# The opening of an attention and feed-forward kernel, its first chunks ordered by hand

## The chip, the cores and the metric

The kernel runs on one core of a Trainium2 chip. The metric is the device time of one execution in microseconds (us), the median of several; lower is better. A core has a matrix engine (TensorE, PE in the profile), a vector engine (VectorE, DVE), an engine for functions (ScalarE, ACT), GpSimd (POOL), which here does little but issue loads, and SyncE (SP), which issues the stores.

## The reference

Attention with a local window and eight global keys for 4 batches of 8 heads, 768 positions of 64 values, followed by a feed-forward network with a squared ReLU on 3072 tokens of 512 values.

```python
scores = scale * np.matmul(q, k.transpose(0, 1, 3, 2))
rel = pos[:, None] - pos[None, :]
is_global = pos[None, :] < 8
is_local = (rel >= 0) & (rel < 96)
dist = np.where(is_global & ~is_local, 96., np.abs(rel))
scores = np.where(is_global | is_local, scores - slopes[h] * dist, -1e9)
a = softmax(scores);  x = (a @ v) as tokens x (heads * 64)
h = np.maximum(x @ w_in, 0.0)          # w_in 512 x 2048
out = (h * h) @ w_out                  # w_out 2048 x 512
```

Inputs and the output are float32; the loads turn the inputs into float16.

## The kernel before

The tokens are cut into 12 chunks of 256 (3 per batch). A chunk `c` has `u = c % 3`; for `u` other than 0 its attention also needs keys and values of the chunk before it and the global ones of its batch's first chunk.

What is done for one chunk:

- `load(c)`: three loads `sq`, `sk`, `sv` (256 KB each as float16) on GpSimd's DMA queue. The weights come on the same queue, `w_in_sb` and `w_out_sb` in four parts of 512 KB each. The queue's order is the order in which the code issues them. A new load waits for the landing of the one eight before it.
- `turn_q(c)`, `turn_k(c)` (together `prep(c)`): eight transposes each on TensorE into PSUM, then a copy out, on ScalarE, or on VectorE in the opening of chunk 0. For `qx` two half-copies follow on VectorE (`beside`). For `kx` with `u` other than 0 four VectorE copies exchange keys (`change`).
- `fix_v(c)`: copies of `sv` into `vodd` and `veven` on VectorE, one copy for `u = 0`, five otherwise.
- `attention(c)` gives eight jobs, `att[c][0..7]`. Jobs 0 and 1 (`both`) compute the scores of two pairs of heads each: 16 matmuls `sp`, four exponentials `ex` on ScalarE, then two products with the decay mask, `phat`, on VectorE. Jobs 2 to 5 (`attend`) are eight matmuls `av` each, then a reciprocal `rec` and a product `tm` on VectorE. Jobs 6 and 7 (`to_x`) are four matmuls `trx` and a cast `xt` on ScalarE. The usual order of the eight is 0, 2, 3, 1, 6, 4, 5, 7.
- `f1(c)`: eight jobs of the first layer, each eight matmuls `hps` (128 x 256), a ReLU `hr` on ScalarE and its square `h` on VectorE.
- `f2(c)`: eight jobs of the second layer, each four matmuls `yps` (128 x 512). They run through two halves of the tokens (j = 0, 1) and four parts of `w_out`. After the fourth job of a half a copy `y` on VectorE and the store follow.

The order of instructions on each engine is written out by hand. A list of main jobs (`f1`, `f2`) is mixed with side jobs by `place(main, side, slots)`: a side job with slot i stands ahead of main job i. `run` goes through such a list. VectorE work that follows a ScalarE result (`phat`, `h`, `beside`, `change`) is put in a list `later` and given out ahead of the next job.

The opening does the attention of chunk 0 and starts that of chunk 1. Then come three mixed lists: `f1(0)` with the attention of chunk 1, `f1(1)` with that of chunk 2, `f2(0)` with that of chunk 3. From there a loop takes for each chunk `c` the jobs of `f2(c)` and `f1(c + 1)` in turn, with the attention of chunk `c + 3` and the preparation of chunk `c + 4` beside them. `warm(n)` is n matmuls on zeros into a bank that nobody reads; before, there is one call with six.

PSUM has six banks in rotation for all of these tiles (`bank`), and two for `yps`. The masks are filled on ScalarE by `fill_decay`: first the part for chunks with `u = 0`, and later the third part, for chunks with `u` other than 0.

Of the kernel before, what the change touches and what calls it, by code (L numbers as in the profile page):

```python
# [10 lines left out]
AF = mybir.ActivationFunctionType  # L11
# [3 lines left out]
P = 128  # L15
# [3 lines left out]
def place(main, side, slots):  # L19

    out = []
    for i in range(len(main) + 1):
        out += [g for g, s in zip(side, slots) if s == i] + main[i:i + 1]
    return out
# [3 lines left out]
def kernel(  # L28
# [73 lines left out]

    def fill_small():
        V = nc.vector
        V.memset(tiny, 0.0)
        nc.scalar.activation(out=tiny, in_=tiny, func=AF.Exp)
        V.memset(zero, 0.0)
        V.memset(fill, BIG)
        V.memset(fill[0:GP, 0:1], float(NL))
        V.memset(fill[HP:HP + GP, 1:2], float(NL))  # L110
        V.memset(shift[0:HP], 0.0)
        V.memset(shift[HP:P], float(CH))
        V.memset(thr[0:HP], 0.0)
        V.memset(thr[HP:P], -float(P - 1))

    def fill_dist():

        V = nc.vector
        V.tensor_scalar(out=ident, in0=jmp, scalar1=0.0, scalar2=None, op0=ALU.is_equal)
        V.tensor_scalar(out=dist[:, 1, 0, :], in0=dist[:, 0, 0, :], scalar1=1.0,  # L120
                        scalar2=None, op0=ALU.subtract)
        V.tensor_scalar(out=dist[:, :, 1, :], in0=dist[:, :, 0, :], scalar1=float(P),
                        scalar2=None, op0=ALU.add)
        V.tensor_scalar(out=dist[:, :, 2, :], in0=dist[:, :, 0, :], scalar1=shift,
                        scalar2=None, op0=ALU.add)
        V.tensor_scalar(out=cut, in0=dist, scalar1=0.0, scalar2=float(NL - 1), op0=ALU.max,
                        op1=ALU.min)
        V.tensor_tensor(out=off, in0=dist, in1=cut, op=ALU.not_equal)
        for k0, k1, f in ((0, 2, 0), (2, 3, 1)):
            V.tensor_scalar(out=off[:, :, k0:k1, :], in0=off[:, :, k0:k1, :],  # L130
                            scalar1=fill[:, f:f + 1], scalar2=None, op0=ALU.mult)
        V.tensor_tensor(out=dist, in0=cut, in1=off, op=ALU.max)

    def fill_decay(k0, k1, h0, h1):
        for h in range(h0, h1):
            nc.scalar.activation(out=mask[:, :, h, k0:k1, :], in_=dist[:, :, k0:k1, :],
                                 func=AF.Exp, scale=-slopes[h])

    def fill_perm():
        nc.vector.tensor_scalar(out=perm, in0=jmp2, scalar1=thr, scalar2=None,  # L140
                                op0=ALU.is_equal)

    def warm(n):
        wps = bank([P, 512], "warm")
        for _ in range(n):
            nc.tensor.matmul(wps, lhsT=zero[:, 0:P], rhs=zero, start=True, stop=True)
# [2 lines left out]

    later = []  # L150

    def run(jobs):
        for job in jobs:
            todo, later[:] = list(later), []
            for f in todo:
                f()
            job()


# [9 lines left out]
    def load(c, *which):  # L169
        ck = chunks[c]  # L170
        for src in which or (q, k, v):
            if src is q:
                dst = ck.sq = stage_p.tile([P, H, P], FP16, name="sq", tag="sq")
            elif src is k:
                dst = ck.sk = stage_p.tile([P, H, P], FP16, name="sk", tag="sk")
            else:
                dst = ck.sv = sv_p.tile([P, H, P], FP16, name="sv", tag="sv")
            nc.gpsimd.dma_start(  # L178
                out=dst, in_=src[ck.b, :, ck.u * CH:(ck.u + 1) * CH, :].rearrange(
                    "h (p e) d -> p h (e d)", e=2))  # L180

    def turn_q(c, h0=0, h1=H, by=None):
        ck = chunks[c]
        if h0 == 0:


            ck.q = qk_p.tile([P, 3, H, P], FP16, name="qx", tag="qx")
        trp = bank([P, H, P], "trq", FP16)
        for h in range(h0, h1):
            nc.tensor.transpose(out=trp[:, h, :], in_=ck.sq[:, h, :], identity=ident)  # L190
        hh = slice(h0, h1)
        (by or nc.scalar.copy)(out=ck.q[:, 1, hh, :], in_=trp[:, hh, :])  # L192

        def beside():
            nc.vector.tensor_copy(out=ck.q[0:HP, 2, hh, :], in_=ck.q[HP:P, 1, hh, :])  # L195
            nc.vector.tensor_copy(out=ck.q[HP:P, 0, hh, :], in_=ck.q[0:HP, 1, hh, :])  # L196
        later.append(beside)

    def turn_k(c, h0=0, h1=H, by=None):
        ck = chunks[c]  # L200
        if h0 == 0:
            ck.k = kx_p.tile([P, H, P], FP16, name="kx", tag="kx")
        trp = bank([P, H, P], "trk", FP16)
        for h in range(h0, h1):
            nc.tensor.transpose(out=trp[:, h, :], in_=ck.sk[:, h, :], identity=ident)  # L205
        hh = slice(h0, h1)
        (by or nc.scalar.copy)(out=ck.k[:, hh, :], in_=trp[:, hh, :])  # L207
        if ck.u == 0:
            ck.keys = (ck.k, ck.k)
        else:  # L210
            pre, zero = chunks[c - 1], chunks[c - ck.u]
            kb = qk_p.tile([P, H, P], FP16, name="kb", tag="kb")
            ck.keys = (kb, ck.k)

            def change():
                nc.vector.tensor_copy(out=kb[:, :, 0:HP], in_=ck.k[:, :, 0:HP])
                nc.vector.tensor_copy(out=kb[:, :, HP + GP:P], in_=pre.k[:, :, HP + GP:P])
                nc.vector.tensor_copy(out=kb[:, :, HP:HP + GP], in_=zero.k[:, :, 0:GP])
                nc.vector.tensor_copy(out=ck.k[:, :, 0:GP], in_=zero.k[:, :, 0:GP])
            later.append(change)  # L220
# [88 lines left out]
    def attention(c):  # L309
        ck = chunks[c]  # L310
        ck.phat, ck.tm = {}, {}

        def both(g):
            score(c, 2 * g)
            score(c, 2 * g + 1)

        return ([lambda: both(0), lambda: both(1)] + [lambda a=a: attend(c, a) for a in range(4)]
                + [lambda: to_x(c, 0), lambda: to_x(c, 1)])
# [47 lines left out]
    def load_w_out(m0, m1):  # L366
        nc.gpsimd.dma_start(
            out=w_out_sb[:, m0:m1, :],
            in_=moe_w_out[m0 * P:m1 * P, :].rearrange("(m p) d -> p m d", p=P))
# [5 lines left out]
    with tc.manual_schedule(engines=engines):  # L375
        fill_small()
        fill_index()
        load(0)
        load_w_in(0, 512)
        load(1)  # L380
        fill_dist()
        for f in range(512, d_ff, 512):
            load_w_in(f, f + 512)
        load(2)
        for m in range(0, NFT, 4):
            load_w_out(m, m + 4)
        load(3)
        fill_decay(0, 2, 0, 8)
        att = [attention(c) for c in range(NC)]
        dve = nc.vector.tensor_copy  # L390
        run([lambda: warm(6), lambda: turn_q(0, 0, 4, dve), lambda: turn_q(0, 4, 8, dve),
             lambda: turn_k(0, 0, 4, dve), lambda: turn_k(0, 4, 8, dve),
             att[0][0], lambda: (fix_v(0), fill_perm()), att[0][1], att[0][2], att[0][3],
             lambda: turn_q(1), att[0][6], lambda: turn_k(1), att[0][4], att[0][5],
             lambda: fix_v(1), att[0][7], lambda: fill_decay(2, 3, 0, 4), att[1][0],
             lambda: fill_decay(2, 3, 4, 8)])
        ORD1 = (2, 3, 1, 6, 4, 5, 7)
        run(place(f1(0), [att[1][i] for i in ORD1] + prep(2) + [lambda: fix_v(2)],
                  [2, 3, 4, 5, 6, 7, 8, 6, 7, 7]))
        load(4)  # L400
        run(place(f1(1), [att[2][i] for i in ORDER] + prep(3) + [lambda: fix_v(3)],
                  [0, 2, 3, 4, 5, 6, 7, 8, 6, 7, 7]))
        load(5)
        run(place(f2(0), [att[3][i] for i in ORDER] + prep(4) + [lambda: fix_v(4)],
                  [0, 2, 3, 4, 5, 6, 7, 8, 6, 7, 7]))
        for c in range(1, NC):
            if c + 5 < NC:
                load(c + 5)
            main = zip_jobs(f2(c), f1(c + 1)) if c + 1 < NC else f2(c)
            side, slots = [], []  # L410
            if c + 3 < NC:
                side = [att[c + 3][i] for i in ORDER]
                slots = [0, 4, 5, 7, 8, 11, 12, 15]
            if c + 4 < NC:
                side += prep(c + 4) + [lambda c=c: fix_v(c + 4)]
                slots += [2, 9, 13]
            run(place(main, side, slots))

# [34 lines left out]
```

The softmax here doesn't subtract the row's maximum and nothing guards it: scores larger than these inputs give would overflow.

## Time and profile before

| | |
|---|---|
| time, median of 3 | 240.07 us (239.79 to 240.2) |
| span of the profiled execution | 239.2 us |
| TensorE busy | 221.9 us (93%) |
| VectorE busy | 152.4 us (64%) |
| ScalarE busy | 143.6 us (60%) |
| GpSimd busy | 38.6 us (16%) |
| first layer, 768 matmuls `hps` | 101.1 us, 276 ns each |
| second layer, 384 matmuls `yps` | 97.3 us, 379 ns each |
| loads on GpSimd's queue | 41664 packets, 13.63 MB |

Matmuls are pipelined, so those of one group overlap and their lengths add up to more than the time in which they run; the distance from one start to the next is what one costs. A busy share is a mean over the whole span, while the stages have different limits. A row of a timeline gives start, length, engine, line, what is written and read, how often, and in brackets the time that the engine stood idle just before and what ended it.

### The profile page before, as it was taken

To read this page: it belongs to the slowest core of one execution; us is meant where nothing else is said; L and a number is where in the kernel's file an instruction comes from. 1 tells how busy PE (TensorE), PEld (TensorE's weight loads), DVE (VectorE), ACT (ScalarE), POOL (GpSimd) and SP (SyncE) were. 2 spreads that over 40 slices of the span, in tenths; PEclk is the share of its full clock that TensorE was granted. 3 is DMA by queue.
4 is the path that set the end of the run, shared out by engine and by line. 5 is a ranking of instruction groups with operands and counts; after the bars stand their busy time and mean duration, and the time that the engine had idled before them with its cause. 6 is when DMAs were issued, how large, how long until landed. Compare 5 with 4: busy or idle time off the path is not lost.

```text
span 239.2 us, 5383 instructions
## 1 busy us (share of the span) xinstructions
PE 221.9 (93%) x2214; PEld 155.1 (65%) x2214; DVE 152.4 (64%) x409; ACT 143.6 (60%) x256; POOL 38.6 (16%) x51
## 2 busy tenths in 40 slices
PE   4666988979899999999999999999999999999993
PEld 1554776846567767777676777767766676766651
DVE  7676689766967765567768755658758564333231
ACT  2975996957755764864764774784684564233310
POOL 8842534212302102102102000000000000000000
PEclk9999999999999999999999999999999999999998
DMA  6999999994968159158249110110110111101112
GB/s 61 192 193 203 192 207 187 182 181 83 167 98 84 51 89 91 48 87 88 57 79 90 44 47 0 47 45 3 44 47 0 47 45 47 43 1 47 44 44 88
DMA packets 45144, 20.26 MB, mean 85 GB/s; under 512 B 37952, under 2 KB 42048, under 8 KB 45120
## 3 DMA queue, kind: packets, MB, share of 16 engines
q0 software_dynamic: 41664, 13.63, 51.0%
q1 hardware_dynamic: 3456, 6.29, 6.8%
q8 instruction: 17, 0.28, 0.5%
q14 instruction: 7, 0.06, 0.1%
HBM read 27.26 MB, written 6.29 MB: 140 GB/s over the span
## 4 chain that ended last, share of the span: by engine, by line
PE 82%; ACT 8%; DVE 6%; DMA 2%; issue 1%; POOL 0%; POOLq 0%
PE yps L341 34%; PE hps L329 33%; PE sp L261 5%; PE av L285 4%; ACT ex L268 4%; PE trx L304 2%; DMA sq<-in_q_dram 2%; PE trq L190 2%; PE trk L205 2%; ACT hr L332 2%; DVE tm L292 1%; ACT kx L207 1%; ACT qx L192 1%; DVE qx L195 1%; DVE qx L196 1%
## 5 line engine op out<-in xcount | busy, mean ns | idle before, releaser
L329 PE MATMUL hps<-xt,w_in_sb 128*128 128x256 f16 x768 | 101.1, 276 | 0.0
L341 PE MATMUL yps<-w_out_sb,h 128*128 128x512 f16 x384 | 97.3, 379 | 0.0
L332 ACT ACTIVATE hr<-hps 128x512 f16<-128x512 f32 x96 | 58.9, 617 | 62.3 <-PE hps L329 58.0
L329 PEld LDWEIGHTS <-w_in_sb 128*128 128x128 f16 x768 | 72.7, 99 | 18.5 <-issue 0.2
L333 DVE TENSOR_TENSOR h<-hr 128x512 f16<-128x512 f16 x96 | 40.5, 422 | 43.9 <-ACT hr L332 43.4
L268 ACT ACTIVATE ex<-sp 128x512 f16<-128x512 f32 x96 | 49.4, 609 | 8.3 <-PE sp L261 8.3
L341 PEld LDWEIGHTS <-h 128*128 128x128 f16 x384 | 34.8, 98 | 26.6
L271 DVE TENSOR_TENSOR phat<-ex,mask 128x1024 f16<-128x1024 f16 x48 | 33.0, 691 | 20.7 <-ACT ex L268 20.7
L285 PEld LDWEIGHTS <-phat 128*128 128x128 f16 x384 | 18.8, 101 | 8.6 <-DVE phat L271 2.0
L292 DVE TENSOR_TENSOR tm<-av,rec 128x256 f16<-128x256 f32 x48 | 20.4, 425 | 1.7
L285 PE MATMUL av<-vodd,phat 128*128 128x65 f16 x256 | 18.5, 201 | 2.5 <-DVE vodd L238 1.5
L345 DVE COPY y<-yps 128x512 f32<-128x512 f32 x24 | 16.4, 685 | 5.4 <-PE yps L341 5.4
L306 ACT CAST xt<-trx 128x512 f16<-128x512 f32 x24 | 14.6, 608 | 8.5 <-PE trx L304 8.5
L261 PE MATMUL sp<-qx,kx 64*128 64x128 f16 x256 | 15.5, 232 | 2.9 <-DVE kx L207 1.3
L178 POOL DMA_DIRECT2D sq<-in_q_dram x12 | 10.7, 892 | 44.6 <-PE trq L190 40.3
L261 PEld LDWEIGHTS <-kx 64*128 64x128 f16 x256 | 10.5, 100 | 9.3 <-issue 6.8
L178 POOL DMA_DIRECT2D sk<-in_k_dram x12 | 10.5, 876 | 33.9 <-PE trk L205 29.1
L304 PE MATMUL trx<-perm,tm 128*128 128x128 f16 x96 | 10.6, 226 | 4.7 <-DVE tm L292 4.7
L304 PEld LDWEIGHTS <-tm 128*128 128x128 f16 x96 | 7.3, 99 | 8.8 <-DVE tm L292 6.2
L192 ACT COPY qx<-trq 128x1024 f16<-128x1024 f16 x11 | 11.6, 1054 | 1.6 <-PE trq L190 1.6
L207 ACT COPY kx<-trk 128x1024 f16<-128x1024 f16 x11 | 11.8, 1069 | 0.8 <-PE trk L205 0.8
L285 PE MATMUL av<-veven,phat 128*128 128x65 f16 x128 | 11.3, 194 | 0.0
(55 smaller groups left out, 132.5 us busy)
## 6 DMA issues: line engine op xcount, KB each, us to landing
out_dram<-y SPq DMA_DIRECT2D x24, 256.0 KB, 2.0
sq<-in_q_dram POOLq DMA_DIRECT2D x12, 256.0 KB, 6.3
sk<-in_k_dram POOLq DMA_DIRECT2D x12, 256.0 KB, 6.9
sv<-in_v_dram POOLq DMA_DIRECT2D x12, 256.0 KB, 7.5
w_in_sb<-in_moe_w_in_dram POOLq DMA_DIRECT2D x4, 512.0 KB, 12.2
w_out_sb<-in_moe_w_out_dram POOLq DMA_DIRECT2D x4, 512.0 KB, 17.2
```

Of the source, the lines that this page charges most:

```text
L178: nc.gpsimd.dma_start(out=dst, in_=src[ck.b, :, ck.u * CH:(ck.u + 1) * CH, :].rearrange("h (p e) d -> p h (e d)", e=2))
L261: nc.tensor.matmul(sp[ek][:, e, s, :], lhsT=ck.keys[rr][rows, h, :], rhs=ck.q[rows, 1 - ek:3 - ek, h, rr * HP:(rr + 1) * HP], start=True, ...
L268: nc.scalar.activation(out=ex[:, ek].rearrange("p e c -> p (e c)"), in_=sp[ek].rearrange("p e s c -> p (e s c)"), func=AF.Exp, scale=scale)
L271: later.append(lambda: nc.vector.tensor_tensor(out=phat, in0=ex, in1=mask[:, :, 2 * a:2 * a + 2, k0:k0 + 2, :].rearrange("p k e s c -> p k ...
L285: nc.tensor.matmul(av[:, e, rr, :], lhsT=phat[:, ek, e, s * P:(s + 1) * P], rhs=ck.vals[rr][:, 2 * a + e, ek, 0:D + 1], start=ek == 0, sto ...
L292: nc.vector.tensor_tensor(out=tm.rearrange("p r e d -> p e r d"), in0=av[:, :, :, 0:D], in1=rec[:, :, :, None].to_broadcast([P, 2, 2, D]), ...
L304: nc.tensor.matmul(trx[:, i, rr, :], lhsT=ck.tm[2 * g + i][:, rr, :, :], rhs=perm, start=True, stop=True)
L329: nc.tensor.matmul(hps[:, m2, :], lhsT=w_in_sb[:, kk, m * P:(m + 1) * P], rhs=ck.xt[:, kk, :], start=kk == 0, stop=kk == NCT - 1)
L332: nc.scalar.activation(out=hr, in_=hps, func=AF.Relu)
L333: later.append(lambda: nc.vector.tensor_tensor(out=ck.h2[:, 2 * i:2 * i + 2, :], in0=hr, in1=hr, op=ALU.mult))
L341: nc.tensor.matmul(ck.yps, lhsT=ck.h2[:, m, j * P:(j + 1) * P], rhs=w_out_sb[:, m, :], start=m == 0, stop=m == NFT - 1)
L345: nc.vector.tensor_copy(out=y, in_=ck.yps)
```

## The change

The first three chunks get a new order. The attention of chunk 0 is written out call by call, with the decay mask's third part in one piece behind the exponentials of chunk 0, and five more `warm` matmuls in two places. The first mixed list is then `f1(0)` and then `f2(0)`, with the attention of chunk 1 alone; the second is `f1(1)`, `f2(1)` and `f1(2)` with the preparations of chunks 2, 3 and 4 and the attentions of chunks 2 and 3. So a chunk's two layers stand one behind the other there. From chunk 2 on the loop is as before but with attention two chunks ahead and preparation three ahead. The loads of `w_out` go ahead of those of chunk 2. Some small VectorE work (`thr`, `ident`, the input of the first exponential) moves to other places.

The aim is to have the feed-forward work start earlier and to spread attention over more of it.

```diff
     def fill_small():
         V = nc.vector
-        V.memset(tiny, 0.0)
-        nc.scalar.activation(out=tiny, in_=tiny, func=AF.Exp)
         V.memset(zero, 0.0)
+        nc.scalar.activation(out=tiny, in_=zero[:, 0:1], func=AF.Exp)
...
-        V.memset(thr[0:HP], 0.0)
-        V.memset(thr[HP:P], -float(P - 1))
     def fill_dist():
-        V.tensor_scalar(out=ident, in0=jmp, scalar1=0.0, scalar2=None, op0=ALU.is_equal)
...
     def fill_perm():
+        nc.vector.memset(thr[0:HP], 0.0)
+        nc.vector.memset(thr[HP:P], -float(P - 1))
...
-        load(2)
         for m in range(0, NFT, 4):
             load_w_out(m, m + 4)
+        load(2)
         load(3)
         fill_decay(0, 2, 0, 8)
+        nc.vector.tensor_scalar(out=ident, in0=jmp, scalar1=0.0, scalar2=None,
+                                op0=ALU.is_equal)
...
-        run([lambda: warm(6), lambda: turn_q(0, 0, 4, dve), lambda: turn_q(0, 4, 8, dve),
-             lambda: turn_k(0, 0, 4, dve), lambda: turn_k(0, 4, 8, dve),
-             att[0][0], lambda: (fix_v(0), fill_perm()), att[0][1], att[0][2], att[0][3],
-             lambda: turn_q(1), att[0][6], lambda: turn_k(1), att[0][4], att[0][5],
-             lambda: fix_v(1), att[0][7], lambda: fill_decay(2, 3, 0, 4), att[1][0],
-             lambda: fill_decay(2, 3, 4, 8)])
-        ORD1 = (2, 3, 1, 6, 4, 5, 7)
-        run(place(f1(0), [att[1][i] for i in ORD1] + prep(2) + [lambda: fix_v(2)],
-                  [2, 3, 4, 5, 6, 7, 8, 6, 7, 7]))
+        warm(6)
+        turn_q(0, 0, 4, dve)
+        flush()
+        turn_q(0, 4, 8, dve)
+        turn_k(0, 0, 4, dve)
+        flush()
+        turn_k(0, 4, 8, dve)
+        fix_v(0)
+        fill_perm()
+        att[0][0]()
+        flush()
+        att[0][1]()
+        fill_decay(2, 3, 0, 8)
+        warm(3)
+        att[0][2]()
+        att[0][3]()
+        att[0][6]()
+        turn_q(1)
+        q1 = later.pop()
+        flush()
+        att[0][4]()
+        att[0][5]()
+        q1()
+        warm(2)
+        att[0][7]()
+        turn_k(1)
+        side = [lambda: fix_v(1)] + [att[1][i] for i in ORDER]
+        run(place(f1(0) + f2(0), side, [0, 2, 5, 6, 8, 9, 11, 12, 14]))
         load(4)
-        run(place(f1(1), [att[2][i] for i in ORDER] + prep(3) + [lambda: fix_v(3)],
-                  [0, 2, 3, 4, 5, 6, 7, 8, 6, 7, 7]))
         load(5)
-        run(place(f2(0), [att[3][i] for i in ORDER] + prep(4) + [lambda: fix_v(4)],
-                  [0, 2, 3, 4, 5, 6, 7, 8, 6, 7, 7]))
-        for c in range(1, NC):
-            if c + 5 < NC:
-                load(c + 5)
+        side = (prep(2) + [lambda: fix_v(2)] + [att[2][i] for i in ORDER]
+                + prep(3) + [lambda: fix_v(3)] + [att[3][i] for i in ORDER]
+                + prep(4) + [lambda: fix_v(4)])
+        run(place(f1(1) + f2(1) + f1(2), side,
+                  [0, 1, 2, 3, 6, 7, 8, 9, 11, 12, 14, 10, 11, 12, 13, 16, 17, 18, 19, 21, 22, 24,
+                   20, 22, 23]))
+        for c in range(2, NC):
+            if c + 4 < NC:
+                load(c + 4)
...
+            if c + 2 < NC:
+                side = [att[c + 2][i] for i in ORDER]
+                slots = [0, 4, 5, 7, 8, 11, 12, 15]
             if c + 3 < NC:
-                side = [att[c + 3][i] for i in ORDER]
-                slots = [0, 4, 5, 7, 8, 11, 12, 15]
-            if c + 4 < NC:
-                side += prep(c + 4) + [lambda c=c: fix_v(c + 4)]
+                side += prep(c + 3) + [lambda c=c: fix_v(c + 3)]
                 slots += [2, 9, 13]
```

More of the change, by code (lines that the diff above doesn't have):

```diff
@@ L150, with flush @@
     later = []
+    def flush():
+        todo, later[:] = list(later), []
+        for f in todo:
+            f()
     def run(jobs):
         for job in jobs:
-            todo, later[:] = list(later), []
-            for f in todo:
-                f()
+            flush()
             job()
@@ L400 @@
+        att[0][3]()
+        att[0][6]()
+        turn_q(1)
+        q1 = later.pop()
+        flush()
+        att[0][4]()
[6 more added lines that the diff above has]
+        run(place(f1(0) + f2(0), side, [0, 2, 5, 6, 8, 9, 11, 12, 14]))
         load(4)
-        run(place(f1(1), [att[2][i] for i in ORDER] + prep(3) + [lambda: fix_v(3)],
-                  [0, 2, 3, 4, 5, 6, 7, 8, 6, 7, 7]))
```

## The prediction

> **What bounds the kernel now.** I read the page's first two parts, then the stage table, then the timelines of TensorE and of GpSimd's DMA queue in the first 62 us.
>
> The page: busy shares, and the span in 40 slices of 6 us.
> ```profile
> PE 221.9 (93%) x2214; PEld 155.1 (65%) x2214; DVE 152.4 (64%) x409; ACT 143.6 (60%) x256; POOL 38.6 (16%) x51
> PE   4666988979899999999999999999999999999993
> DMA  6999999994968159158249110110110111101112
> ```
> TensorE is busy from about the eleventh slice on. What can still be gained lies before 62 us, where the DMA row is also full.
>
> The stage table: length, then busy us of each engine.
> ```profile
> core 0: us, PE busy (x) PEld busy (x) DVE busy (x) ACT busy (x) POOL busy (x), PEclk, DMA share, GB/s
> 26.40:49.90 23.50, 19.71 (x279) 16.59 (x277) 19.68 (x55) 19.68 (x36) 9.51 (x11) 1.00 1.57 192
> 49.90:61.90 12.00, 10.95 (x122) 6.21 (x120) 8.31 (x24) 7.37 (x14) 2.71 (x3) 1.00 1.05 120
> 79.50:97.07 17.57, 17.57 (x187) 12.48 (x186) 10.68 (x27) 11.40 (x22) 2.63 (x3) 1.00 0.55 76
> 97.07:114.63 17.56, 17.56 (x185) 12.47 (x186) 12.75 (x35) 11.38 (x22) 2.62 (x3) 1.00 0.55 76
> ```
> Later stages are a chunk every 17.56 us with no idle TensorE. In 26.4 to 49.9 TensorE idles 3.8 us while VectorE and ScalarE are each busy 84%: one attention beside eight short first-layer jobs is too dense for them.
>
> The timeline of TensorE: start, length, what, and idle time before it.
> ```profile
> 9.79 1.56 PE L261 MATMUL sp<-qx,kx 64*128 64x128 f16 x25 [1.31 <-DVE kx L207]
> 20.14 0.40 PE L304 MATMUL trx<-perm,tm 128*128 128x128 f16 x2 [1.69 <-DVE tm L292]
> 21.99 3.59 PE L329 MATMUL hps<-xt,w_in_sb 128*128 128x256 f16 x16
> 27.08 1.03 PE L329 MATMUL hps<-xt,w_in_sb 128*128 128x256 f16 x8
> 39.24 0.24 PE L285 MATMUL av<-vodd,phat 128*128 128x65 f16 x2 [0.99 <-ACT hr L332]
> 49.11 0.29 PE L304 MATMUL trx<-perm,tm 128*128 128x128 f16 x2 [1.48 <-DVE tm L292]
> 61.36 0.23 PE L261 MATMUL sp<-qx,kx 64*128 64x128 f16 x2 [0.67 <-ACT xt L306]
> ```
> Sixteen `hps` matmuls from 21.99 take to 25.37 (the next line's start there), 0.21 us each; from 27.08 eight take to 28.04 with a switch in them, elsewhere in the critical chain 0.87, so 0.108 each. Before some 26 us TensorE runs at half rate, which the page's clock row does not show. The wait at 61.36 is the last one; after it nothing delays TensorE.
>
> The queue on GpSimd: a DMA issue waits for the landing of the one eight before it.
> ```profile
> 22.34 0.74 POOL L367 DMA_DIRECT2D w_out_sb<-in_moe_w_out_dram  x1 [3.04 <-DMA w_in_sb<-in_moe_w_in_dram]
> 24.80 0.89 POOL L178 DMA_DIRECT2D sq<-in_q_dram  x1 [1.72 <-DMA w_in_sb<-in_moe_w_in_dram]
> ...
> 29.17 0.87 POOL L178 DMA_DIRECT2D sq<-in_q_dram  x1 [0.42 <-PE sp L261]
> ...
> 39.52 0.87 POOL L178 DMA_DIRECT2D sk<-in_k_dram  x1 [1.62 <-DMA w_out_sb<-in_moe_w_out_dram]
> ```
> So `w_in`'s third and fourth parts have landed by 22.3 and 24.8, chunk 2 by 29.2, the last of `w_out` by 39.5 (the issue follows its landing by 0.2 to 0.5; I take 39.0).
>
> [...] landings follow the order of issue, so order alone sets when `w_out` is there. [...] the copy `qx<-qx` at 47.20 takes 0.84 us beside a DMA issue, otherwise 0.42.
>
> **The change part by part.**
> 1. The first 10 us. `tiny`, the two `thr` memsets and `ident` leave the front of VectorE: three memsets at 0.1 and `ident` at 0.11 (distance to the next start) are 0.4, so the decay masks start on ScalarE at 5.35 in place of 5.75. `kx` of heads 0 to 3 now goes ahead of the second pair of `qx` half-copies (0.7), so the first scores start near 9.1 in place of 9.79. ScalarE ends the masks at 9.6, and the eight `ex` (4.03 for 8) run 9.7 to 13.7.
> 2. Attention of chunk 0. All eight small masks now stand behind those `ex` on ScalarE: 2.7 us (1.33 and 1.35 before), to 16.4. Queued behind them are the first `xt` cast, `qx` and the second `xt` cast. TensorE reaches the second `trx` only at about 17.6: `phat` of pairs 2 and 3 stand behind two `rec`/`tm` on VectorE and end at 15.2 and 15.9, two `av` at half rate end at 16.75, `rec` and `tm` follow. So the masks are hidden. The five extra `warm` matmuls cost 0.43 each at half rate (the distance from one start to the next among the first six), 2.1 in all. I put 0.5 of it on the path, since they stand where TensorE waits for `phat` and `tm`. First `hps` at 19.0, against 21.99 before less the 0.97 of scores that then stood ahead: 21.0. Two us earlier.
> 3. Clock. [...]
> 4. Transfers. The three transfers of chunk 2 (24.8 to 29.2, 4.35 us) leave the front of `w_out`, so its last part lands at 39.0 - 4.35 = 34.7, and the third at about 32. Chunk 2 lands at 36.1 to 39.1.
> 5. First run of jobs: `f1(0)` and `f2(0)`, with the attention of chunk 1. One job is 0.868 (eight `hps` or four `yps`), `both` 0.55, `attend` 0.25, `to_x` 0.22. The twelfth job (the last of `w_out`, j = 0) is reached after 11 x 0.868 + 2 x 0.55 + 3 x 0.25 + 0.22 = 11.6 of full-rate work. From 19.0, with 4 us at half rate (2.0 lost), that is 32.6; with half rate to 26.4 it is 34.3. Both lie before 34.7: here TensorE waits for `w_out`, a new wait, 0.4 to 2.1 long. ScalarE and VectorE have under 14 us of work in these 17, so they hide. After it: 5 x 0.868 + 0.25 + 0.22 = 4.8. The run ends at 39.5.
> 6. Second run: 24 jobs, chunk preparations 2, 3 and 4, attentions 2 and 3: 24 x 0.868 = 20.8; preparations 3 x 0.89 = 2.7; attentions 2 x (2 x 0.55 + 4 x 0.25 + 2 x 0.22) = 5.1; and the 0.24 by which 17.56 exceeds such a sum for a chunk, twice: 0.5. Together 29.1, to 68.6 with no wait.
>    Waits there, from pitches in this trace (`hr` and `ex` 0.49, a 1024-wide copy 0.9, `phat` 0.61, `rec` with `tm` 0.55, `fix_v` 2.2): the scores of chunk 2 wait 0.3 for the exchange of keys. `attend` waits 0.5 to 1.0, since `phat` stands behind `fix_v` (in 39.24 above it is the same 0.99). The last `to_x` of chunk 3 waits 0.4 and the scores of chunk 4 another 0.4, since ScalarE has two `qk` copies, a cast and six `hr` in some 7 us. Copies beside DMA issues add about 0.4. Sum 2.2, so the run ends at 70.8.
> 7. From there the loop starts at chunk 2 with attention two chunks ahead in place of three. `xt` is then made one stage before its use: its cast has 0.87 + 0.55 + 0.87 = 2.3 us of TensorE work to hide behind and needs about 0.9. No cost. The end of the kernel is the same.
>
> Sum. At 61.36 the kernel before had done 24 jobs and all that the second run's end has done but 16 jobs; 16 x 0.868 = 13.9, so it would have stood there at 75.2. Against 70.8: 4.4 us gained, 240.07 - 4.4 = 235.6.
>
> **The rivals.**
> A. The waits of the second run vanish, because the middle third (`f2(1)`) has no `hr` for ScalarE. For it: 49.9 to 61.9 idles 1.05 against 3.8 in the stretch before. Against it: `fix_v` ahead of `phat` stands as before. Gain 75.2 - 68.6 = 6.6: 233.4.
> B. The second run is as dense as 26.4 to 49.9, where 3.8 of 23.5 us idle. The same share of 29.1 busy us (29.1 x 3.8/19.7) is 5.6, not 2.2. For it: two attentions and three preparations fall on 24 jobs. Against it: a third of the jobs are second-layer ones. Gain 6.6 - 5.6 = 1.0: 239.1.
> C. Slower. The opening gains nothing, `hps` starts at 21.0 and the full clock comes only at 29.8 [...]: the twelfth job is reached at 21.0 + 11.6 + 4.4 = 37.0, 2.3 later than taken, and with the 5.6 of rival B the gain is 6.6 - 2.3 - 5.6 = -1.3: 241.4. For it: fillers are extra work and the masks stand ahead of `xt`. Against it: every part of the opening has slack to 34.7.
>
> **How the numbers follow.** Forecast 0.5, A 0.2, B 0.23, C 0.07. The predicted time is the forecast's 235.6. Unknown are the waits of the second run (0 to 5.6) and the landing of `w_out` (34.5 to 35.1, by where in its issue mark it landed). The range from 233.0 to 239.0 takes in A and the faster half of B, and leaves out C, B's slower half and what lies below A: some 2 in 10. Slower 0.05, the same 0.03, faster 0.92.
>
> **What would show it.** Right: first scores near 9.1, first `hps` near 19, a TensorE wait of 0.4 to 2.1 at the fourth `yps` job that ends near 34.7 with that run of jobs over at 39.5, the second run from there to about 71 with one or two waits of up to 1 us each for `phat` behind `fix_v`, and no wait after about 72. Wrong: no wait for `w_out` (the opening was later than worked out), waits over 4 us between 40 and 70, new waits at the start of each later chunk (the shorter lead costs), or half rate past 27.

## The result, and the profile after

| | before | after |
|---|---|---|
| time, median | 240.03 us | 235.88 us |
| ratio, 95% interval | | 0.9845 [0.9802, 0.9887] |
| span of the profiled execution | 239.2 us | 235.5 us |

The change gains 4.15 us (240.03 - 235.88), beside 4.4 predicted. Both profiled executions are longer than their kernel's median, by 1.0 and 1.4 us (241.05 and 237.25 us timed).

The page after: busy shares, the span in 40 slices of 5.9 us, and the granted clock.
```profile
PE 221.1 (94%) x2219; PEld 153.4 (65%) x2219; DVE 150.6 (64%) x408; ACT 143.2 (61%) x256; POOL 38.8 (16%) x51
PE   4788859999999999999999999999999999999993
PEclk9999997999999999999999999999999999999999
```
TensorE is now busy for 80% or more of each slice from the third to the last but one, except the sixth (29 to 35 us), which is a new hole; in the seventh the clock is down. Neither was there before.

The stage table after: length, busy us of each engine, and the clock as a share.
```profile
core 0: us, PE busy (x) PEld busy (x) DVE busy (x) ACT busy (x) POOL busy (x), PEclk, DMA share, GB/s
26.40:39.50 13.10, 9.35 (x70) 4.62 (x68) 4.10 (x10) 3.33 (x8) 4.39 (x5) 0.87 1.52 194
39.50:70.80 31.30, 30.66 (x359) 23.20 (x357) 22.54 (x61) 23.85 (x42) 7.89 (x9) 1.00 1.11 133
73.00:90.50 17.50, 17.50 (x186) 12.40 (x185) 13.90 (x38) 11.26 (x20) 2.63 (x3) 1.00 0.66 76
90.50:108.00 17.50, 17.50 (x185) 12.41 (x184) 10.45 (x26) 11.34 (x21) 2.63 (x3) 1.00 0.60 92
```
From 26.4 to 39.5 TensorE idles 3.75 of 13.1 us while VectorE and ScalarE are busy for less than a third of it and loads still come in at 194 GB/s: a wait for loads. From 39.5 to 70.8 it idles only 0.6 of 31.3, where the kernel before idled 3.8 of 23.5 and then 1.05 of 12. The later stages are as full as before.

The timeline of TensorE after:
```profile
9.03 2.36 PE L262 MATMUL sp<-qx,kx 64*128 64x128 f16 x32 [0.55 <-DVE kx L208]
14.62 0.61 PE L191 MATMUL trq<-ident,sq 128*128 128x128 f16 x8
17.43 0.38 PE L330 MATMUL hps<-xt,w_in_sb 128*128 128x256 f16 x2
...
29.36 1.02 PE L342 MATMUL yps<-w_out_sb,h 128*128 128x512 f16 x4 [0.86 <-DMA w_out_sb<-in_moe_w_out_dram]
32.02 1.02 PE L342 MATMUL yps<-w_out_sb,h 128*128 128x512 f16 x4 [1.63 <-DMA w_out_sb<-in_moe_w_out_dram]
...
34.55 1.86 PE L342 MATMUL yps<-w_out_sb,h 128*128 128x512 f16 x4 [1.26 <-DMA w_out_sb<-in_moe_w_out_dram]
...
40.85 0.61 PE L191 MATMUL trq<-ident,sq 128*128 128x128 f16 x8
...
45.06 0.23 PE L262 MATMUL sp<-qx,kx 64*128 64x128 f16 x2 [0.54 <-DVE h L334]
...
71.49 0.23 PE L262 MATMUL sp<-qx,kx 64*128 64x128 f16 x2 [0.43 <-DVE kx L220]
```
The same eight transposes in the kernel before:
```profile
14.49 1.04 PE L190 MATMUL trq<-ident,sq 128*128 128x128 f16 x8
```
The eight transposes at 14.62 take 0.61 us against 1.04: the full clock is already there. Then three `yps` jobs in a row wait for their parts of `w_out`, 3.75 us in all, each part landing 2.5 to 2.7 us after the one ahead of it. The job at 34.55 takes 1.86 in place of 1.02: in this execution the profile's record of the granted clock shows half clock for 3.4 us from 34.3 on, which is within the last of the three waits. The scores at 71.49 are those that in the kernel before stand at 61.36, but by then 16 jobs more are done: 61.36 + 13.9 = 75.2, so 3.7 us are gained, as the spans say. Nothing is gained or lost behind this place: from there to the end it is 164.0 us in both.

### The profile page after: what moved, and what is told of

Its sections match the earlier page's. It is cut to its first block, busy times and chain, and to the rows that moved or that the text cites. A ratio compares the mean times of both kernels' runs of the same rounds, so it can differ in the third digit from the quotient of the medians.

```text
span 235.5 us, 5396 instructions
## 1 busy us (share of the span) xinstructions
PE 221.1 (94%) x2219; PEld 153.4 (65%) x2219; DVE 150.6 (64%) x408; ACT 143.2 (61%) x256; POOL 38.8 (16%) x51
## 4 chain that ended last, share of the span: by engine, by line
PE 79%; DMA 12%; DVE 3%; ACT 2%; POOL 2%; issue 1%; POOLq 0%
PE yps L342 35%; PE hps L330 30%; DMA w_out_sb<-in_moe_w_out_dram 8%; PE sp L262 5%; PE av L286 4%; DMA sk<-in_k_dram 4%; PE trx L305 2%; PE trq L191 2%; PE trk L206 2%; ACT ex L269 1%; POOL sq L179 1%; ACT hr L333 1%; DVE tm L293 1%; DVE h L334 1%; ACT kx L208 0%
## 5 line engine op out<-in xcount | busy, mean ns | idle before, releaser
L342 PE MATMUL yps<-w_out_sb,h 128*128 128x512 f16 x384 | 98.3, 383 | 3.8 <-DMA w_out_sb<-in_moe_w_out_dram 3.8
L330 PE MATMUL hps<-xt,w_in_sb 128*128 128x256 f16 x768 | 98.5, 273 | 0.3 <-ACT xt L307 0.2
L333 ACT ACTIVATE hr<-hps 128x512 f16<-128x512 f32 x96 | 58.3, 614 | 56.2 <-PE hps L330 52.6
L330 PEld LDWEIGHTS <-w_in_sb 128*128 128x128 f16 x768 | 71.8, 98 | 16.2 <-issue 0.4
L346 DVE COPY y<-yps 128x512 f32<-128x512 f32 x24 | 16.4, 685 | 11.4 <-PE yps L342 11.4
L307 ACT CAST xt<-trx 128x512 f16<-128x512 f32 x24 | 14.7, 613 | 13.4 <-PE trx L305 13.4
L262 PE MATMUL sp<-qx,kx 64*128 64x128 f16 x256 | 15.0, 229 | 2.0 <-DVE kx L208 0.6
L179 POOL DMA_DIRECT2D sk<-in_k_dram x12 | 10.7, 889 | 36.3 <-PE trk L206 31.3
L179 POOL DMA_DIRECT2D sv<-in_v_dram x12 | 10.8, 902 | 4.5 <-DMA w_in_sb<-in_moe_w_in_dram 2.2
L291 DVE RECIPROCAL rec<-av 128x4 f32<-128x4 f32 x48 | 8.4, 175 | 4.1 <-PE av L286 4.0
```

The source lines that it names most:

```text
L179: nc.gpsimd.dma_start(out=dst, in_=src[ck.b, :, ck.u * CH:(ck.u + 1) * CH, :].rearrange("h (p e) d -> p h (e d)", e=2))
L262: nc.tensor.matmul(sp[ek][:, e, s, :], lhsT=ck.keys[rr][rows, h, :], rhs=ck.q[rows, 1 - ek:3 - ek, h, rr * HP:(rr + 1) * HP], start=True, ...
L307: nc.scalar.copy(out=ck.xt[:, 2 * g:2 * g + 2, :].rearrange("p a c -> p (a c)"), in_=trx.rearrange("p a r c -> p (a r c)"))
L330: nc.tensor.matmul(hps[:, m2, :], lhsT=w_in_sb[:, kk, m * P:(m + 1) * P], rhs=ck.xt[:, kk, :], start=kk == 0, stop=kk == NCT - 1)
L333: nc.scalar.activation(out=hr, in_=hps, func=AF.Relu)
L342: nc.tensor.matmul(ck.yps, lhsT=ck.h2[:, m, j * P:(j + 1) * P], rhs=w_out_sb[:, m, :], start=m == 0, stop=m == NFT - 1)
```

## Experiments

All are compared with the kernel before in the same session (240.18 us in the first four, 240.14 in the others).

| kernel | time us | ratio to before, 95% interval |
|---|---|---|
| changed, `w_out` behind chunk 2 again | 240.6 | 1.0021 [1.0007, 1.0035] |
| changed, `f2(0)` part by part | 233.42 | 0.9716 [0.9694, 0.9737] |
| changed, no extra `warm` | 236.84 | 0.9854 [0.9828, 0.9879] |
| changed, old opening | 235.73 | 0.9819 [0.9798, 0.984] |
| new opening alone | 238.28 | 0.992 [0.9894, 0.9945] |
| before, `w_out` ahead of chunk 2 | 247.3 | 1.0293 [1.0252, 1.0334] |
| changed, old opening, `f2(0)` part by part | 235.35 | 0.9805 [0.977, 0.9841] |
| changed, `warm` in the waits for `w_out` | 235.88 | 0.9833 [0.9788, 0.9877] |

**The order of loads undone.**
```diff
-        for m in range(0, NFT, 4):
-            load_w_out(m, m + 4)
         load(2)
+        for m in range(0, NFT, 4):
+            load_w_out(m, m + 4)
```


> The changed kernel with one part undone: chunk 2's loads stand ahead of w_out again. Theory (the landing of w_out's last part sets when the first run of jobs ends): the last part lands near 39.0 in place of 34.5, the fourth yps job waits till then, and the time is 235.9 + 4.4 = 240.3 us (239.3 to 241.5). Rival (the wait is slack, the dense second run sets the end): under 237.

Measured 240.6 us. The timeline of TensorE of this kernel:
```profile
31.46 1.73 PE L342 MATMUL yps<-w_out_sb,h 128*128 128x512 f16 x4 [4.00 <-DMA w_out_sb<-in_moe_w_out_dram]
...
38.94 1.02 PE L342 MATMUL yps<-w_out_sb,h 128*128 128x512 f16 x4 [1.24 <-DMA w_out_sb<-in_moe_w_out_dram]
...
43.72 0.61 PE L191 MATMUL trq<-ident,sq 128*128 128x128 f16 x8
```
The last part is used at 38.94 where 34.55 was, 4.4 later, and the whole gain is gone. The run of jobs ends 4.8 after that (43.72), as the sum of its jobs says. So the landing of `w_out` sets the end of the first run; without its place in the queue the new lists are worth nothing. The clock record of this kernel shows the full clock only from 18.0 on, though the opening is that of the changed kernel, and half clock again from 31.6 to 35.1, after the wait of 4.00 us (1.73 for the four `yps` at 31.46). Neither moved the last part: TensorE waited for it all the same.

**The same move in the kernel before.** Here only the loads of chunk 2 go behind `w_out`.

> The kernel before with only the loads of w_out moved ahead of chunk 2. Theory: the old lists need chunk 2 at 31 and w_out only at 50, so the first transpose of chunk 2 waits until about 36 and nothing is gained: 243 to 246 us. Rival (loads are hidden either way): 239.5 to 240.7.

Measured 247.3 us, beyond the range. The timeline of TensorE of this kernel:
```profile
37.12 1.03 PE L190 MATMUL trq<-ident,sq 128*128 128x128 f16 x8 [5.65 <-DMA sq<-in_q_dram]
```
The first transpose of chunk 2 waits 5.65 us, until 37.12, about 1 later than expected, and then the eight run at half clock (1.03), which was not in the sum. The place in the queue is right only together with the new lists.

**The old opening under the new lists.** The calls of the opening as in the kernel before (the small VectorE work stays where the change put it), then `f1(0)` and `f2(0)` with the rest of chunk 1's attention in slots 5 to 14.

> The changed kernel with the opening in its old order (as the kernel before up to the first list), the rest as changed. Theory: hps starts near 21 to 22 with half clock to about 26, the fourth yps job is reached near 34.5 to 35.5, where w_out lands anyway: 235.8 to 237 us. Rival (the opening by hand is the gain): its 3 to 4 us are lost, 238.5 to 240.

Measured 235.73 us, just below the range and the same as the changed kernel; the profiled execution took 236.56. The timeline of TensorE of this kernel:
```profile
21.92 6.76 PE L330 MATMUL hps<-xt,w_in_sb 128*128 128x256 f16 x40
...
35.36 1.02 PE L342 MATMUL yps<-w_out_sb,h 128*128 128x512 f16 x4
...
40.15 0.61 PE L191 MATMUL trq<-ident,sq 128*128 128x128 f16 x8
```
It reaches `hps` 4.5 us later (21.92 against 17.43), and the first 40 are at half clock in large part: 6.8 us where 40 x 0.108 = 4.3 is the full rate (the clock record has the full clock from 26.5 on). It gets to the last part of `w_out` at 35.36 without any wait, and ends the run at 40.15. So with this order of jobs the opening by hand buys only waiting: its head start ends at the landing of `w_out`.

**The new opening under the old lists.** The changed kernel up to `turn_k(1)`, then the lists, the loop and the loads of the kernel before, with all of chunk 1's attention inside `f1(0)`.

> The new opening alone: the changed kernel's first part up to turn_k(1), then the old lists, the old loop and the old order of loads, with all of chunk 1's attention inside f1(0). Theory: no job of the old lists is bound by w_out, so an opening that ends 3 us earlier at full clock carries through, less some 1.3 us in which the preparation of chunk 3 waits for its loads: 235 to 237.5 us. Rival (the old lists are bound by ScalarE and VectorE, which take it back): 238 to 240.

Measured 238.28 us, above the range of the theory and within that of the rival, near its fast end: 1.86 gained (240.14 - 238.28). The timeline of TensorE of this kernel, then its stage table:
```profile
17.84 1.21 PE L330 MATMUL hps<-xt,w_in_sb 128*128 128x256 f16 x8
...
23.01 0.24 PE L286 MATMUL av<-vodd,phat 128*128 128x65 f16 x2 [1.44 <-DVE phat L272]
...
46.34 0.28 PE L305 MATMUL trx<-perm,tm 128*128 128x128 f16 x2 [1.48 <-DVE tm L293]
```
```profile
17.50:31.00 13.50, 11.02 (x157) 9.21 (x154) 10.50 (x31) 10.78 (x20) 4.99 (x6) 1.00 1.43 198
31.00:44.00 13.00, 10.73 (x151) 9.00 (x149) 11.05 (x33) 10.60 (x20) 5.24 (x6) 1.00 1.53 194
```
It starts `hps` 3.2 us earlier (17.84 against 21.0 worked out for before), at full clock (the clock record has it from 15.6 on). But TensorE idles 4.75 us in these 26.5, with VectorE and ScalarE each busy some 80%, and the waits it shows are for `phat` and `tm`: lists with a whole attention to eight first-layer jobs take back a large part of the head start. The time is the rival's, though 1.86 us are kept. The theory's wait of chunk 3's preparation for its loads did not come.

**`f2(0)` part by part.** Both halves of the tokens take a part of `w_out` before the next part is needed. The two banks for `yps` are enough.
```diff
+    def f2_parts(c):
+        return [lambda j=j, m0=m0: second(c, j, m0) for m0 in range(0, NFT, 4)
+                for j in range(2)]
...
-        run(place(f1(0) + f2(0), side, [0, 2, 5, 6, 8, 9, 11, 12, 14]))
+        run(place(f1(0) + f2_parts(0), side, [0, 2, 5, 6, 8, 9, 11, 12, 14]))
```


> The changed kernel with f2(0) going through w_out part by part, both halves of the tokens for each part, so that the last part is needed at the seventh job in place of the fourth. Theory: of the 3.8 us of waits for w_out under 0.8 are left, and no clock drop follows them: 232.0 to 233.2 us. Rival (ScalarE and VectorE take the time back in the second run, which is as dense as before): waits there grow by 2 or more, and the time is 234.5 to 236.

Measured 233.42 us, 0.2 above the range and the fastest of all. The timeline of TensorE of this kernel:
```profile
29.66 1.02 PE L343 MATMUL yps<-w_out_sb,h 128*128 128x512 f16 x4 [0.25 <-DMA w_out_sb<-in_moe_w_out_dram]
...
34.70 1.89 PE L343 MATMUL yps<-w_out_sb,h 128*128 128x512 f16 x8 [0.42 <-DMA w_out_sb<-in_moe_w_out_dram]
36.42 0.61 PE L191 MATMUL trq<-ident,sq 128*128 128x128 f16 x8
...
67.70 0.23 PE L262 MATMUL sp<-qx,kx 64*128 64x128 f16 x2 [0.43 <-DVE kx L220]
```
Of 3.75 us of waits 0.7 are left, the clock stays up (1.89 for the eight `yps` at 34.70), and the run ends at 36.42. The second run takes 31.3 (67.70 - 36.42) against 30.6 in the changed kernel (71.49 - 40.85), 0.6 given back where the rival wanted 2 or more.

**Part by part under the old opening.**

> The old opening with the changed lists and with f2(0) part by part. Theory: with the old opening no job waited for w_out, so the order of parts changes nothing: 235.4 to 236.2 us, and the new opening is worth some 2.3 us once w_out is out of the way (233.4). Rival (the order of parts helps by itself): 233 to 234.5.

Measured 235.35 us, just below the range; its interval overlaps that of the old opening with `f2(0)` in its order. So the order of parts by itself does nothing that these runs can tell. With it the new opening is worth 1.9 us (235.35 - 233.42), without it nothing (235.73 against 235.88).

**No extra `warm`.** The two calls `warm(3)` and `warm(2)` are left out.

> The changed kernel without the five extra warm matmuls. Theory: [...] the first hps about as early, and the 3.8 us of waits for w_out shrink by what is lost: 235.3 to 236.4 us. Rival (the fillers' early clock is what gives the gain): 237.5 to 239.

Measured 236.84 us, between the ranges; its interval overlaps that of the changed kernel. The timeline of TensorE of this kernel:
```profile
13.78 1.06 PE L191 MATMUL trq<-ident,sq 128*128 128x128 f16 x8
...
17.38 2.06 PE L330 MATMUL hps<-xt,w_in_sb 128*128 128x256 f16 x16
...
34.62 1.86 PE L342 MATMUL yps<-w_out_sb,h 128*128 128x512 f16 x4 [1.27 <-DMA w_out_sb<-in_moe_w_out_dram]
```
At 13.78 the clock is still half, and full only from 17.1 on; `hps` starts as early as with the fillers, and the last part of `w_out` is used within 0.1 us of the changed kernel. The trace gives no time to the fillers. This execution has the drop to half clock at the fourth `yps` job too, and two of the four took 237.2, as the changed kernel's execution with the drop did (237.25). The other two took 236.12 and 236.44, 0.1 to 0.9 above the changed kernel's executions of 235.57 to 236.02; whether the fillers are worth that stays open.

**`warm` in the waits.** Three, six and five `warm` matmuls ahead of the second, third and fourth `yps` job.

> The changed kernel with 3, 6 and 5 warm matmuls in the three waits for w_out (0.65, 1.3 and 1.1 us of work in 0.86, 1.63 and 1.26 us of waiting). Theory: w_out still sets the end of the run of jobs, but the clock never drops after the waits: no execution shows a half-rate window near 35, and the time is 235.4 to 235.9 us in all. Rival (the drop has another cause): a half-rate window in some executions, up to 237.5.

Measured 235.88 us, with executions from 235.6 to 236.62, two of them (235.94 and 236.62) above the range and in that of the rival; whether those had a stretch at half rate no trace shows. The timeline of TensorE of this kernel:
```profile
32.94 1.24 PE L144 MATMUL warm<-zero 128*128 128x512 f16 x5
34.61 1.02 PE L342 MATMUL yps<-w_out_sb,h 128*128 128x512 f16 x4 [0.18 <-DMA w_out_sb<-in_moe_w_out_dram]
...
39.40 0.61 PE L191 MATMUL trq<-ident,sq 128*128 128x128 f16 x8
...
70.03 0.23 PE L262 MATMUL sp<-qx,kx 64*128 64x128 f16 x2 [0.43 <-DVE kx L220]
```
The job at 34.61 takes 1.02 again and the run ends at 39.40, 1.45 before that of the profiled changed kernel: this is what the half clock cost there. The median is not lower. Of the six executions of the changed kernel on record two took 237.25 (the profiled one) and 237.49 us and four 235.57 to 236.02, so going by the time the drop is not in most of them, though all of them wait for `w_out`. That `warm` prevents it is not shown by one trace.

## Why the prediction was right

- The first 10 us. Scores at 9.03 (9.1 predicted), `ex` from 9.67 (9.7). Right.
- Attention of chunk 0. The first two `hps` come at 17.43 and the rest from 18.04, not from 19.0. This step made the chain too long: the last `phat` of chunk 0 ends at 15.6 where 15.9 was taken, and the last `trx` starts at 16.86 in place of some 17.6. The early clock is only a part of it: at half clock until 18.0, in the kernel with `w_out` behind chunk 2 again, `hps` starts at 18.20, and without the fillers, at half clock until 17.1, at 17.38.
- The clock. The step failed. Step 5 takes half rate for 4 us from 19.0, so to 23, or to 26.4; the 4 us were the author's estimate, and no trace shows them. In the trace of the kernel before the full rate is there from 26.1 on by its clock record, not from 26.4. In the changed kernel it came at 13.8, and in others with this opening at 13.4 (`f2(0)` part by part), 15.6 (under the old lists) and 18.0 (`w_out` behind chunk 2 again), at 17.1 without the fillers, but with the old opening at 25.3 to 26.5. So the new order of the opening brings it, at a time that differs by 4.6 us (18.0 - 13.4) among these executions; which part of that order does it stays open. Both errors cost nothing, for the earlier start went into the wait for `w_out`.
- Transfers. The last part of `w_out` is used at 34.55 (34.7 predicted). Right, and the undone order shows that this landing carries the gain: moving three transfers on GpSimd's queue moved the use of the last part by 4.4 us, where 4.35 was worked out.
- First run of jobs. One wait of 0.4 to 2.1 was predicted, at the fourth `yps` job. There it was 1.26, but the second and third waited too, 3.75 in sum, since TensorE came to the second at 28.5, 2 to 4 us before the time that the forecast gives it (30.6 to 32.3). The end at 39.5 was right without a clock drop (39.40 with `warm` in the waits); with one it is 40.85.
- Second run. 29.1 without waits and 2.2 of waits were predicted, to 70.8; it takes 30.6, and ends 0.7 later only because it starts 1.35 later. The term for the waits was mis-sized: TensorE is busy 29.56 of these 30.64, so 1.1 of waits came in place of 2.2. Of these 0.54 are for the exchange of keys (put down to `h`, which ends with the last of its copies, at 44.9) and 0.43 for that of chunk 4; that of `attend` for `phat` behind `fix_v` did not come.
- The shorter lead costs nothing: 17.50 us a chunk, against 17.56 before.
- Rivals. The 1.1 of waits in the second run lie midway between A's none and the forecast's 2.2. B's 5.6 is refuted by them. C did not happen: with the old opening `hps` starts at 21.92, later than C says, but the full clock comes at 26.5 and not at 29.8 (the author's estimate, shown by no trace), and the time is that of the changed kernel.

The total. In the profiled execution the second run starts 1.35 later than predicted and is 0.7 shorter, so 3.7 us are gained in place of 4.4. Where the clock stays up, as with `warm` in the waits, the same scores of chunk 4 start at 70.03, which is 5.2 before 75.2. But 75.2 is worked out from an execution of the kernel before that took 1.0 us more than its median. With that taken off, 4.2 are left, near the medians' 4.15. The forecast took its 4.4 from this longer execution and from a second run taken 0.7 too long: these two errors nearly cancel, so that the number came within 0.3 us is in part luck. The mechanism is the one predicted: `w_out`'s landing ends the first run, and the second runs nearly full.

## What to carry to other kernels

In an opening that is bound by loads, work out when the last piece of each input lands, and order the jobs by it: a hand-tuned start that runs into the next landing buys nothing until the job that needs it moves back. Here the new opening was worth nothing until each weight part was taken for both halves of the tokens, and 1.9 us then. The new lists with the new order of loads gave the whole gain under the old opening too. They idle less: 1.1 us in their second run, where the new opening under the old lists idled 4.75 in 26.5. A likely reason is that attention now also stands beside second-layer jobs, which use neither ScalarE nor much of VectorE (in the changed kernel the copies `y` are 16.4 of its 150.6 us). The lists change in several ways at once, and no run separates these.

## What was not expected of the hardware

The clock of TensorE dropped to half for 3.4 us, beginning in the last of three waits of 0.86, 1.63 and 1.26 us within 6.1 us (28.5 to 34.55), with work between them, while a single wait of 1.48 us in the kernel before (at 49.11) left it up. It also fell at two longer single waits: at that of 4.00 us, with `w_out` behind chunk 2 again, to half from 31.6 to 35.1, and at that of 5.65 us, with `w_out` ahead under the old lists, after which the eight transposes took 1.03 us where 0.61 is the full rate. In the changed kernel no single wait was that long, and going by their time most of its executions had no drop; what decides stays open.
